# Seven quarter products for eight: one level of Strassen's algorithm in tiles three to nine of a chunked attention and feed-forward kernel

## The chip, the cores and the metric

The kernel runs on one core of a Trainium2 chip. The metric is the device time of one execution in microseconds (us). A core has a matrix engine (TensorE, PE in the profile, with its weight loads as PEld), VectorE (DVE), ScalarE (ACT), GpSimd (POOL) and SyncE (SP). Matmuls write to PSUM, in banks of 128 partitions by 512 floats; the other operands live in SBUF; DMA queues move data between SBUF and DRAM.

## The reference

Attention is computed in chunks of 64 tokens for 8 batches, 8 heads, 576 tokens and a head width of 64. Its output, seen as 4608 tokens by 512 features, goes through a feed-forward block of 2048 hidden units:

```python
scores = (1 / sqrt(64)) * matmul(q_c, k_c.T)          # 64 x 64 in each chunk
attn = exp(scores - max(scores)); attn = attn / (sum(attn) + 1e-09)
x = matmul(attn, v_c)                                 # as 4608 x 512
h = x @ w_in                                          # 512 x 2048
g = where(h >= 1, h, where(h <= -1, 0, (h + 1)**2 / 4))
out = g @ w_out                                       # 2048 x 512
```

The feed-forward weights come in as 64-bit floats; everything else is float32.

## The kernel before

**Tiles.** Tokens are worked in nine tiles of 512 (`NTILE`, `T`). In each tile there are four attention groups of two heads (`NP`) and 16 blocks of 128 hidden units (`NF`). Features run down the partitions: x of a tile is four blocks of 128 features by 512 tokens, one from each attention group.

**Precision.** Matmuls work on a reduced format (float32r), so each operand is split into a high part (a cast, on ScalarE) and a low part (the difference, on VectorE). A product is three matmuls: high by high, high by low, low by high. The split of x is `attn_split` (L513 to L526), that of the hidden units `ffn_split` (L554), and that of the weights happens once, in `prepare` (L250 to L294), which also turns 64-bit floats into 32-bit ones. All 16 + 16 prepared weight blocks stay in SBUF.

**The feed-forward block.** `ffn_in` (L529) does, for a block j, 12 matmuls of 512 columns (four feature blocks by three products, L539) into one of two PSUM banks `ps_h`; then ScalarE (L546, L549) and VectorE (L550) compute the activation. `ffn_out` (L564) runs two blocks behind (`LAG`): for each of four slices of 128 tokens three matmuls (L574), accumulated over the 16 blocks in four PSUM banks `ps_o`. `store` (L584) drains these and sends them out.

**Attention** of a group is prepared one or two groups ahead: 32-by-32 turns of q and k on VectorE (L375; in tile 0 on TensorE), scores (L399), softmax on VectorE and ScalarE (`attn_softmax`, L444), a DMA that finishes the turn of the weights (L499; on SyncE's queue, in tile 1 on GpSimd's), then the values product (L421), and the split of x for the next tile.

**Order.** Nothing is issued directly: every step is `plan.add(engine, cost, ...)`, with what it reads and writes. `Plan.emit` (L61) then walks a model of the engines in time and puts each engine's instructions into a fixed order: of the steps that are ready on an engine, the one added first goes first. On the chip each engine then runs its queue strictly in that order, and waits where data are not there. Queues are those of TensorE, ScalarE, VectorE, GpSimd (in tiles 0 and 1 some loads and transfers) and SyncE (all other DMAs). The filler matmuls of the start (L717, L720) keep TensorE busy while the first data arrive.

**The main loop** (L670 on) goes over tiles t and blocks j; the weights are prepared during tile 0, two at each j.

Of the kernel before, what the change touches and what calls it, by code (L numbers as in the profile page):

```python
# [17 lines left out]
class Plan:  # L18
# [8 lines left out]

    def __init__(self):
        self.parts = []
        self.writer = {}  # L30
        self.readers = {}

    def add(
        self, engine, cost, emit, reads=(), writes=(), lag=0.0, columns=0, port=False, moving=0.0
    ):
# [25 lines left out]
    def emit(self, filler):  # L61
# [25 lines left out]
        for _ in range(len(parts)):  # L87
            while True:
                best = None
                for e in engines:  # L90
                    while soon[e] and soon[e][0][0] <= free[e]:
                        heapq.heappush(now[e], heapq.heappop(soon[e])[1])
                    if now[e]:
                        start = free[e]
                    elif soon[e]:
                        start = soon[e][0][0]
                    else:
                        continue
                    if best is None or start < best[0]:
                        best = start, e  # L100
                start, e = best
                if filling and free[fill_engine] < start and fill_emit():
                    free[fill_engine] = self.products_end(free[fill_engine], fill_cost, fill_columns)
                    continue
                break
            while soon[e] and soon[e][0][0] <= start:
                heapq.heappush(now[e], heapq.heappop(soon[e])[1])
            n = heapq.heappop(now[e])
# [21 lines left out]
def kernel(  # L130
# [53 lines left out]
    xh_bufs = [buffers(sb, f"xh{g}_", 2, F32R) for g in range(NP)]  # L184
    xl_bufs = [buffers(sb, f"xl{g}_", 2, F32R) for g in range(NP)]
    r_bufs = buffers(sb, "r", 2)
    gh_bufs, gl_bufs = buffers(sb, "gh", 2, F32R), buffers(sb, "gl", 2, F32R)
    tmp_bufs = buffers(sb, "tmp", 4)
# [322 lines left out]
            plan.add(queue, 4.8, move, (xkey,), (akey,), lag=1.7, moving=0.4)  # L511

    def attn_split(t, g):  # L513
        pkeys, pair = bank_pair_of(t, g)
        hkey, xh = xh_bufs[g][t % 2]
        lkey, xl = xl_bufs[g][t % 2]

        def of_tokens(x):
            split = "p (r n q) -> p r n q" if t == 0 else "p (n r q) -> p r n q"
            return x.rearrange(split, r=2, q=C)  # L520

        ps = pair[:, :, HALF:].rearrange("p r (n q) -> p r n q", q=C)
        plan.add("act", 0.48, lambda: nc.scalar.copy(out=of_tokens(xh), in_=ps), pkeys, (hkey,))  # L523
        plan.add("dve", 0.6, lambda: nc.vector.tensor_tensor(  # L524
            out=of_tokens(xl), in0=ps, in1=of_tokens(xh.bitcast(F32)), op=ALU.subtract
        ), (*pkeys, hkey), (lkey,))  # L526
# [27 lines left out]
    def ffn_split(t, j):  # L554
        n = t * NF + j
        rkey, r = r_bufs[n % 2]
        ghkey, gh = gh_bufs[n % 2]
        glkey, gl = gl_bufs[n % 2]
        plan.add("act", 0.52, lambda: nc.scalar.copy(out=gh, in_=r), (rkey,), (ghkey,))  # L559
        plan.add("dve", 0.6, lambda: nc.vector.tensor_tensor(  # L560
            out=gl, in0=r, in1=gh.bitcast(F32), op=ALU.subtract
        ), (rkey, ghkey), (glkey,), port=True)

    def ffn_out(t, j):  # L564
        n = t * NF + j
        ghkey, gh = gh_bufs[n % 2]
        glkey, gl = gl_bufs[n % 2]
        for s in range(NS):
            pkey, acc = o_banks[s]

            def products(s=s, acc=acc):
                cols = slice(s * P, (s + 1) * P)
                for i, (x, half) in enumerate(((gh, 0), (gh, 1), (gl, 0))):
                    nc.tensor.matmul(  # L574
# [9 lines left out]
    def store(t, s):  # L584
# [15 lines left out]

        plan.add("sp", 0.6, send, (okey,), (), lag=1.7, moving=0.8)


    order = [("wi", 0), ("wi", 1)]
    for j in range(NF):
# [61 lines left out]
        11: ((back, 2),), 13: ((back, 3), (front, 4)),  # L667
    }
    LAG = 2
    for t in range(NTILE + 1):  # L670
        for j in range(NF):
            n = (t + 1) * NP + j // 4

            def attention():
# [5 lines left out]
                if j % 4 == 2:  # L680
                    if n + 1 < ALL:
                        attn_products(values_of(*now), scores_of(*then), lag=0.8)
                        attn_split(*now)
                        attn_softmax(*then)
# [8 lines left out]
                    what(*divmod(NP + g, NP))  # L693
            else:
                attention()
            if t < NTILE:
                ffn_in(t, j)
            prepare_next()
            prepare_next()
            m = t * NF + j - LAG  # L700
            if 0 <= m < NTILE * NF:
                ffn_out(*divmod(m, NF))
            if t < NTILE:
                ffn_split(t, j)

    zeros = place("zeros", "wo", 11, [P, 2, T], F32R)[:, 0, :]
    nc.vector.memset(zeros.bitcast(F32), 0.0)
# [60 lines left out]
```

## Time and profile before

| what | us |
|---|---|
| median of three runs | 877.92 (877.04 to 878.34) |
| the profiled execution | 879.29 |
| its span, first to last instruction | 877.5 |
| TensorE busy in the span | 858.6 |
| VectorE, ScalarE, GpSimd busy | 454.0, 377.6, 31.0 |
| matmuls of the h products (L539), high and low x | 384.0 and 224.5 |
| matmuls of the output products (L574), high and low | 356.0 and 224.3 |

Busy time of groups of matmuls overlaps, since one begins while the one before still drains. The mean granted TensorE clock is 0.997. In the profile's rows of groups stand line, engine, operation, out<-in, shapes and count, then busy time and mean duration in ns, then idle time before them and what ended it. DMA moved 63.94 MB in all, GpSimd's own queue 2.10 MB of it.

### The profile page before, as it was taken

What the parts mean: (1) busy time and instruction counts of PE and PEld (TensorE: products, weight loads), DVE (VectorE), ACT (ScalarE), POOL (GpSimd) and SP (SyncE); (2) the same over time, 40 slices, a digit from 0 to 9 for tenths busy, and PEclk for the clock granted to TensorE, in tenths of its full rate; (3) what the DMA queues carried; (4) which work ended last, traced back from release to release, by engine and by line L of the source; (5) the groups of instructions that cost most, each with busy time, mean ns of one, the idle gap of its engine ahead of it and who ended that gap; (6) DMA issues with size and microseconds to landing.
All of it is one profiled execution on the core that took longest, in us unless ns stands there. A gap on an engine that the chain in (4) does not pass through costs nothing.

```text
span 877.5 us, 15042 instructions
## 1 busy us (share of the span) xinstructions
PE 858.6 (98%) x5918; PEld 705.0 (80%) x5918; DVE 454.0 (52%) x775; ACT 377.6 (43%) x691; POOL 31.0 (4%) x58
## 2 busy tenths in 40 slices
PE   6998999999999999999999999999999999999998
PEld 6777778888888888888888888888888888888886
DVE  4899998444444445444544454444444444423222
ACT  4888875333433333333433343333333433333332
POOL 5123100000000000000000000000000000000000
PEclk9999999999999999999999999999999999999999
DMA  9889924222322223222322233222222311001001
GB/s 215 219 249 239 246 37 105 48 42 46 87 49 49 49 49 97 49 49 49 96 49 46 46 80 62 47 43 78 52 47 43 79 37 25 13 1 49 0 1 49
DMA packets 207304, 63.94 MB, mean 73 GB/s; under 512 B 184448, under 2 KB 199808, under 8 KB 207232
## 3 DMA queue, kind: packets, MB, share of 16 engines
q1 hardware_dynamic: 204640, 60.60, 29.9%
q0 software_dynamic: 1536, 2.10, 0.9%
q8 instruction: 47, 0.77, 0.4%
q10 hardware_dynamic: 1056, 0.26, 0.2%
q14 instruction: 25, 0.20, 0.1%
HBM read 45.09 MB, written 9.44 MB: 62 GB/s over the span
## 4 chain that ended last, share of the span: by engine, by line
PE 86%; DVE 6%; SPq 3%; DMA 2%; ACT 1%; issue 1%; DVEq 0%; ACTq 0%
PE ps_h L539 42%; PE ps_o L574 41%; PE ps_a L421 2%; SPq L308 2%; PE ps_a L399 2%; DVE tmp L271 1%; DVE tmp L276 1%; DMA words_wi<-in_moe_w_in_dram 1%; SPq L239 1%; DMA q_sb<-in_q_dram 1%; DVE parts_wo L290 1%; DVE tmp L264 1%; DVE r L550 1%; DVE gl L560 0%; DVE parts_wi L290 0%
## 5 line engine op out<-in xcount | busy, mean ns | idle before, releaser
L539 PE MATMUL ps_h<-xh,parts_wi 128*128 128x512 f32 x1152 | 384.0, 393 | 0.8 <-DVE parts_wi L290 0.4
L574 PE MATMUL ps_o<-parts_wo,gh 128*128 128x512 f32 x1152 | 356.0, 390 | 0.0
L539 PEld LDWEIGHTS ps_h<-xh,parts_wi 128*128 128x128 f32 x1152 | 216.1, 188 | 48.0 <-DVE parts_wi L290 0.9
L574 PEld LDWEIGHTS ps_o<-parts_wo,gh 128*128 128x128 f32 x1152 | 216.6, 188 | 45.2 <-DVE parts_wo L290 0.2
L550 DVE SCALAR_TENSOR_TENSOR r<-ps_h,r 128x512 f32<-128x512 f32 x144 | 97.8, 679 | 263.5 <-ACT r L549 263.5
L539 PE MATMUL ps_h<-xl,parts_wi 128*128 128x512 f32 x576 | 224.5, 390 | 0.0
L574 PE MATMUL ps_o<-parts_wo,gl 128*128 128x512 f32 x576 | 224.3, 389 | 0.0
L546 ACT ACTIVATE r<-ps_h 128x512 f32<-128x512 f32 x144 | 86.3, 599 | 266.0 <-PE ps_h L539 266.0
L559 ACT CAST gh<-r 128x512 fp32r<-128x512 f32 x144 | 89.7, 623 | 153.4 <-PE ps_o L574 113.3
L560 DVE TENSOR_TENSOR gl<-r,gh 128x512 fp32r<-128x512 f32 x144 | 98.2, 682 | 108.0 <-ACT gh L559 108.0
L574 PEld LDWEIGHTS ps_o<-parts_wo,gl 128*128 128x128 f32 x576 | 108.4, 188 | 22.5
L539 PEld LDWEIGHTS ps_h<-xl,parts_wi 128*128 128x128 f32 x576 | 108.2, 188 | 21.4
L549 ACT ACTIVATE r<-r 128x512 f32<-128x512 f32 x144 | 91.1, 632 | 3.4
L523 ACT CAST xh<-ps_a 128x512 fp32r<-128x512 f32 x34 | 20.0, 589 | 39.7 <-DVE mx L455 39.2
L421 PEld LDWEIGHTS ps_a<-aT,v_sb 64*64 64x64 f32 x1056 | 19.2, 136 | 15.5 <-issue 10.2
L480 DVE TENSOR_REDUCE sm<-e 128x8 f32<-128x512 f32 x30 | 20.6, 686 | 21.2 <-ACT e L474 20.3
L421 PE MATMUL ps_a<-aT,v_sb 64*64 64x64 f32 x1056 | 23.7, 227 | 4.1 <-ACT e L464 4.1
L524 DVE TENSOR_TENSOR xl<-ps_a,xh 128x512 fp32r<-128x512 f32 x34 | 23.5, 690 | 1.7 <-ACT xh L523 0.8
L455 DVE TENSOR_REDUCE mx<-ps_a 128x8 f32<-128x512 f32 x34 | 23.4, 688 | 0.6 <-PE ps_a L399 0.5
L507 DVE STREAM_TRANSPOSE x<-e 128x512 f32<-128x512 f32 x32 | 22.7, 710 | 0.9
L399 PE MATMUL ps_a<-kT,qT 64*64 64x64 f32 x1056 | 21.6, 219 | 1.2 <-DVE kT L375 1.2
L375 DVE STREAM_TRANSPOSE qT<-q_sb 128x512 f32<-128x512 f32 x32 | 22.4, 701 | 0.0
(80 smaller groups left out, 400.0 us busy)
## 6 DMA issues: line engine op xcount, KB each, us to landing
words_wi<-in_moe_w_in_dram SPq DMA_DIRECT2D x16, 512.0 KB, 5.8
words_wo<-in_moe_w_out_dram SPq DMA_DIRECT2D x16, 512.0 KB, 6.3
v_sb<-in_v_dram SPq DMA_DIRECT2D x128, 64.0 KB, 2.4
out_dram<-tmp SPq DMA_DIRECT2D x32, 256.0 KB, 2.0
q_sb<-in_q_dram SPq DMA_DIRECT2D x112, 64.0 KB, 2.4
k_sb<-in_k_dram SPq DMA_DIRECT2D x112, 64.0 KB, 2.4
aT<-x SPq DMA_DIRECT2D x224, 32.0 KB, 1.9
aT<-x POOLq DMA_DIRECT2D x32, 32.0 KB, 5.6
```

Source lines behind the costliest of these rows:

```text
L399: nc.tensor.matmul(out=pair[i * C:(i + 1) * C, half, place:place + C], lhsT=qT[rows, at], rhs=kT[rows, at], start=True, stop=True,)
L421: nc.tensor.matmul(out=pair[h * C:(h + 1) * C, half, HALF + n * C:HALF + (n + 1) * C], lhsT=v_sb[rows, of:of + C], rhs=aT[rows, at:at + C] ...
L455: plan.add("dve", 0.6, lambda: nc.vector.tensor_reduce(out=mx4, in_=sc, axis=AX.X, op=ALU.max), pkeys, (mkey,))
L507: plan.add("dve", 0.6, lambda: nc.vector.transpose(out=x.rearrange("p (e c q) -> p c e q", e=2, q=Q), in_=e.rearrange("p (c e q) -> p c e ...
L524: plan.add("dve", 0.6, lambda: nc.vector.tensor_tensor(out=of_tokens(xl), in0=ps, in1=of_tokens(xh.bitcast(F32)), op=ALU.subtract), (*pkey ...
L539: nc.tensor.matmul(out=ps, lhsT=weight["wi", j][:, half, kc * P:(kc + 1) * P], rhs=x, start=(kc == 0 and i == 0), stop=(kc == KC - 1 and i ...
L546: plan.add("act", 0.48, lambda: nc.scalar.activation(out=r, in_=ps, func=AF.Relu, bias=0.5, scale=0.5), (pkey,), (rkey,))
L549: plan.add("act", 0.52, lambda: nc.scalar.square(out=r, in_=r), (), (rkey,))
L550: plan.add("dve", 0.6, lambda: nc.vector.scalar_tensor_tensor(out=r, in0=ps, scalar=1.0, in1=r, op0=ALU.max, op1=ALU.min), (pkey,), (rkey,))
L559: plan.add("act", 0.52, lambda: nc.scalar.copy(out=gh, in_=r), (rkey,), (ghkey,))
L560: plan.add("dve", 0.6, lambda: nc.vector.tensor_tensor(out=gl, in0=r, in1=gh.bitcast(F32), op=ALU.subtract), (rkey, ghkey), (glkey,), port ...
L574: nc.tensor.matmul(out=acc, lhsT=x[:, cols], rhs=weight["wo", j][:, half, :], start=(j == 0 and i == 0), stop=(j == NF - 1 and i == 2),)
```

## The change

In tiles 2 to 8 ("three to nine") the product h = x @ w_in is done by one level of Strassen's algorithm in Winograd's form. A pair of hidden blocks (2p, 2p + 1) and the tile's 512 tokens are cut in two by two: hidden blocks in two, tokens in two halves of 256, features in even and odd groups of 128 (so that each half is two blocks of 128 features). Instead of eight quarter products there are seven, each of some sum of weight quarters by some sum of x quarters.

- **Weights.** In tile 1 `combine_weights` forms the four sums of quarters of a pair on VectorE, splits them into high and low parts in two staging tiles, and GpSimd's queue writes all seven operands of the pair (three are unsummed quarters) to DRAM: 8 pairs x 7 DMAs of 256 KB.
- **Reuse of SBUF.** The weight blocks `wi0` to `wi15` are handed over, two after each pair: to sets of x operands, to five ring slots of 512 KB, to a tile for h, one for partial sums, and a third buffer for the hidden units.
- **Streaming.** In tiles 2 to 8 each ring slot holds the weights of two products; `load_combos` loads it on GpSimd's queue, 196 times.
- **x.** `combine_x` takes the place of `attn_split` for tiles 2 on: a copy from PSUM to SBUF, sums of halves on VectorE, and their splits, 256 or 512 wide. It is added to the plan after the next group's softmax, not before.
- **Products.** `quarter` does six matmuls of 256 columns into one of the two `ps_h` banks. `ffn_quad` runs the seven of a pair, each drained by one addition on VectorE with a partial sum in SBUF (the first by a copy on ScalarE, the sixth by two additions), and puts the eight output groups of the pair before among them. The activation now reads h from SBUF.
- **Order.** `plan.add` gets `ahead`: a step with it goes before steps that were added up to that many places earlier. The additions and the copy have 100.

```diff
         self.parts.append((engine, cost, emit, needs, lag, columns, port, moving, writes))
+        self.turn.append((n - ahead, n))
...
-                        heapq.heappush(now[e], heapq.heappop(soon[e])[1])
+                        heapq.heappush(now[e], self.turn[heapq.heappop(soon[e])[1]])
...
     def attn_split(t, g):
+        if t > 1:
+            combine_x(t, g)
+            return
...
+    RING = 5
...
+    def combine_x(t, g):
+        i = g // 2
...
+        act_copy(
+            0.48, lambda: raw[name]().rearrange("p (n r q) -> p r n q", r=2, q=C), lambda: ps,
+            pkeys, (name,),
+        )
+        sub = ALU.subtract
+        if g % 2 == 0:
+            dve(0.34, sub, part(ta, 0), part(xe, 1), part(xe, 0), ("xe",), ("ta",))
+            act_copy(0.3, part(h0, 0), part(xe, 0), ("xe",), (h0k,))
+            act_copy(0.3, part(h0, 1), part(ta, 0), ("ta",), (h0k,))
+            dve(0.34, sub, part(l0, 0), part(xe, 0), plain(part(h0, 0)), ("xe", h0k), (l0k,))
+            dve(0.34, sub, part(l0, 1), part(ta, 0), plain(part(h0, 1)), ("ta", h0k), (l0k,))
+            return
+        dve(0.34, sub, part(tb, 0), part(xo, 1), part(ta, 0), ("xo", "ta"), ("tb",))
+        dve(0.34, sub, part(tb, 1), part(xo, 1), part(xe, 1), ("xo", "xe"), ("tb",))
+        dve(0.34, sub, part(ta, 1), part(xo, 0), part(tb, 0), ("xo", "tb"), ("ta",))
+        act_copy(0.52, h1, xo, ("xo",), (h1k,))
+        dve(0.6, sub, l1, xo, plain(h1), ("xo", h1k), (l1k,))
+        act_copy(0.52, h2, tb, ("tb",), (h2k,))
+        dve(0.6, sub, l2, tb, plain(h2), ("tb", h2k), (l2k,))
+        act_copy(0.3, part(m, 0), part(ta, 1), ("ta",), (mk,))
+        dve(0.34, sub, part(m, 1), part(ta, 1), plain(part(m, 0)), ("ta", mk), (mk,))
+
+    def combine_weights(p):
...
+        for j, ks, key, w in zip(js, keys, (k1, k2), (w1, w2)):
+            dve(0.6, ALU.add, fixed(w), lambda j=j: weight["wi", j][:, 0, :].bitcast(F32),
+                lambda j=j: weight["wi", j][:, 1, :].bitcast(F32), ks, (key,))
...
+        dve(0.34, ALU.add, fixed(two(s12, 0)), fixed(a21), fixed(a22), (k2,), (k12,))
+        dve(0.34, ALU.subtract, fixed(two(s12, 1)), fixed(two(s12, 0)), fixed(a11), (k1,), (k12,))
+        dve(0.34, ALU.subtract, fixed(two(s34, 0)), fixed(a11), fixed(a21), (k1, k2), (k34,))
+        dve(0.34, ALU.subtract, fixed(two(s34, 1)), fixed(a12), fixed(two(s12, 1)), (k1, k12), (k34,))
+        for n, (key, ap) in enumerate(((k12, s12), (k34, s34))):
...
+            act_copy(0.52, fixed(hi), fixed(ap), (key,), (hkey,))
+            dve(0.6, ALU.subtract, fixed(lo), fixed(ap), fixed(hi.bitcast(F32)), (key, hkey), (lkey,))
...
+        for r, src, reads in (
+            (0, of_block(0, 0), keys[0]), (1, of_block(0, 1), keys[0]), (6, of_block(1, 1), keys[1]),
+            (2, of_stage(0, 1), st[0]), (3, of_stage(0, 0), st[0]),
+            (5, of_stage(1, 0), st[1]), (4, of_stage(1, 1), st[1]),
+        ):
...
+                nc.gpsimd.dma_start(out=dst.bitcast(F32), in_=ap.bitcast(F32))
+
+            plan.add("pool", 0.7, send, reads, (f"dram{d}_{n}",), lag=1.7, moving=0.8)
+
+    def load_combos(d):
...
+            nc.gpsimd.dma_start(
+                out=held[ap].bitcast(F32), in_=combos[d % len(combos)].bitcast(F32)
+            )
...
+        plan.add("pool", 0.8, emit, (f"dram{n}_0", f"dram{n}_1"), (key,), lag=1.7, moving=1.5)
+
+    def quarter(t, p, r):
+        step = (t - 2) * NQ * 7 + 7 * p + r
+        d, n = divmod(step, 2)
+        while loaded["n"] < min(d + RING, LOADS):
+            load_combos(loaded["n"])
+            loaded["n"] += 1
+        pkey, ps = h_banks[step % 2]
...
+            w = held[f"ring{d % RING}"][:, n, :]
+            for i, (_, hi, lo) in enumerate(ops):
+                for k, (x, y) in enumerate(((0, hi), (0, lo), (1, hi))):
+                    at = (2 * x + i) * P
+                    nc.tensor.matmul(
+                        out=ps[:, :QC], lhsT=w[:, at:at + P], rhs=y(),
+                        start=i == 0 and k == 0, stop=i == 1 and k == 2,
+                    )
+
+        plan.add("pe", 0.72, emit, (f"ring{d % RING}", *(k for ks, _, _ in ops for k in ks)), (pkey,),
+                 columns=6 * QC)
...
+    def ffn_quad(t, p):
...
+        def add(out, product, name):
+            (pkey, ps), (skey, ap), (okey, o) = product, snap(name), into(out)
+            plan.add("dve", 0.36, lambda: nc.vector.tensor_tensor(
+                out=o(), in0=ps, in1=ap(), op=ALU.add
+            ), (pkey, skey), (okey,), ahead=100)
...
+        product = quarter(t, p, 0)
+        key, ap = snap("a")
+        act_copy(0.3, ap, fixed(product[1]), (product[0],), (key,), ahead=100)
+        add("h00", quarter(t, p, 1), "a")
+        out_products(2)
+        add("u", quarter(t, p, 2), "a")
+        out_products(1)
+        add("w", quarter(t, p, 3), "u")
+        out_products(1)
+        add("h01", quarter(t, p, 4), "w")
+        activate(0)
+        out_products(1)
+        product = quarter(t, p, 5)
+        add("v", product, "u")
+        add("h11", product, "w")
+        out_products(2)
+        add("h10", quarter(t, p, 6), "v")
+        activate(1)
+        out_products(1)
...
+            if t == 1:
...
+                if j % 2 == 1:
+                    combine_weights(j // 2)
+                    hand_over(j - 1)
+                    hand_over(j)
```

More of the change, by code (lines that the diff above doesn't have):

```diff
@@ L29, in __init__ @@
         self.parts = []
+        self.turn = []
         self.writer = {}
@@ L33, in add @@
     def add(
-        self, engine, cost, emit, reads=(), writes=(), lag=0.0, columns=0, port=False, moving=0.0
+        self, engine, cost, emit, reads=(), writes=(), lag=0.0, columns=0, port=False, moving=0.0,
+        ahead=0,
     ):
@@ L556, in ffn_split, with high, low, ffn_out @@
         rkey, r = r_bufs[n % 2]
[L557 to L568, printed above, removed]
+        ghkey, _, glkey, _ = g_of(t, j)
+        def high():
+            nc.scalar.copy(out=g_of(t, j)[1], in_=r)
+        def low():
+            _, gh, _, gl = g_of(t, j)
+            nc.vector.tensor_tensor(out=gl, in0=r, in1=gh.bitcast(F32), op=ALU.subtract)
+        plan.add("act", 0.52, high, (rkey,), (ghkey,))
+        plan.add("dve", 0.6, low, (rkey, ghkey), (glkey,), port=True)
+    def ffn_out(t, j, *some):
+        ghkey, _, glkey, _ = g_of(t, j)
+        for s in some or range(NS):
             pkey, acc = o_banks[s]
             def products(s=s, acc=acc):
+                _, gh, _, gl = g_of(t, j)
                 cols = slice(s * P, (s + 1) * P)
@@ L601, in store, with take, emit @@
         plan.add("sp", 0.6, send, (okey,), (), lag=1.7, moving=0.8)
+    QC = T // 2
+    NQ = NF // 2
+    RING = 5
+    held = {}
+    def take(name, tags, shape, dtype, keys):
+        old = [f"{w}{j}_{n}" for w, j in tags for n in range(2)] if tags[0][0] == "wi" else list(tags)
+        def emit():
+            tag = f"{tags[0][0]}{tags[0][1]}" if tags[0][0] == "wi" else tags[0]
+            held[name] = sb.tile(shape, dtype, name=name, tag=tag)
+        plan.add("pool", 0.0, emit, (), (*old, *keys))
@@ new lines, in unit, with fixed @@
+    def unit(name, n):
+        return lambda: held[name][:, n, :]
+    def fixed(ap):
+        return lambda: ap
+    raw = {}
+    for g, name in enumerate(("xe", "xo", "ta", "tb")):
+        raw[name] = lambda name=name: held[name]
+    SNAPS = {"a": (0, 0), "u": (0, 1), "v": (1, 0), "w": (1, 1)}
+    units = [[], []]
+    for i in range(7):
+        units[0] += [(f"x0_{2 * i + n}", unit(f"set{i}", n)) for n in range(2)]
+    units[1] = [
+        *((f"xh{g}_1", fixed(xh_bufs[g][1][1])) for g in range(NP)),
+        *((f"xl{g}_1", fixed(xl_bufs[g][1][1])) for g in range(NP)),
+        *((f"xl{g}_0", fixed(xl_bufs[g][0][1])) for g in range(NP)),
+        ("x1_0", unit("set7", 0)), ("x1_1", unit("set7", 1)),
+    ]
@@ new lines, in act_copy, with dve, part, plain @@
+    def act_copy(cost, out, src, reads, writes, ahead=0):
+        plan.add(
+            "act", cost, lambda: nc.scalar.copy(out=out(), in_=src()), reads, writes, ahead=ahead
+        )
+    def dve(cost, op, out, one, two, reads, writes):
+        plan.add("dve", cost, lambda: nc.vector.tensor_tensor(
+            out=out(), in0=one(), in1=two(), op=op
+        ), reads, writes, port=True)
+    def part(ap, n):
+        return lambda: ap()[:, cols(n)]
+    def plain(ap):
+        return lambda: ap().bitcast(F32)
@@ L604, with g_of @@
+    def g_of(t, j):
+        n = t * NF + j
+        if t < 2:
+            return *gh_bufs[n % 2], *gl_bufs[n % 2]
+        if n % 3 < 2:
+            return *gh_bufs[n % 3], *gl_bufs[n % 3]
+        return "gh2", held.get("g3") and held["g3"][:, 0, :], "gl2", held.get("g3") and held["g3"][:, 1, :]
     order = [("wi", 0), ("wi", 1)]
@@ L695 @@
                 attention()
-            if t < NTILE:
-                ffn_in(t, j)
+            if t > 1 and j % 2 == 0:
+                p = j // 2
+                if t < NTILE:
+                    ffn_quad(t, p)
+                elif j == 0:
+                    for n in range(2):
+                        ffn_out(t - 1, NF - 2 + n)
+            if t > 1:
+                continue
+            ffn_in(t, j)
             prepare_next()
```

124 lines of the change are left out of this document (116 added, 8 removed).

## Prediction

> **What bounds the kernel now.** I read the page's list of engines first, then a table by stage, then the chain that ended last for one round of the steady part.
>
> ```profile
> span 877.5 us, 15042 instructions
> PE 858.6 (98%) x5918; PEld 705.0 (80%) x5918; DVE 454.0 (52%) x775; ACT 377.6 (43%) x691; POOL 31.0 (4%) x58
> ...
> 30.00:134.00 104.00, 96.83 (x745) 77.41 (x744) 101.07 (x192) 85.98 (x204) 16.98 (x33) 0.98 0.73 190
> 134.00:226.50 92.50, 92.50 (x643) 76.02 (x642) 50.00 (x84) 35.99 (x61) 0.00 (x0) 1.00 0.31 65
> 226.50:318.80 92.30, 92.30 (x642) 75.86 (x641) 44.56 (x75) 34.56 (x58) 0.00 (x0) 1.00 0.26 55
> ...
> 562.38 2.95 PE ps_h L539 x12
> 565.33 2.72 PE ps_o L574 x12
> 568.05 2.72 PE ps_h L539 x12
> ...
> 585.46 2.95 PE ps_h L539 x12
> ```
>
> The columns of the stage rows are length, then PE, PEld, DVE, ACT and POOL busy, granted clock, DMA share and GB/s. The first row is tile 0: VectorE is busy 101.07 of 104 us there, preparing weights. Then come tile 1 and tile 2: TensorE is busy all the time, VectorE about half. The chain is nothing but matmuls: 12 for h (L539, 2.72 us), 12 for the output (L574, 2.72 us), in turn. A round (four h blocks and one attention group) lasts 585.46 - 562.38 = 23.08 us, so a tile 92.3 us. Tiles 2 to 8, which the change rewrites, hold the time from about 226.5 us to the end: 651 us. So matmul time counts at its full price there, and work on other engines costs nothing until it makes TensorE wait.
>
> **The h products.** One block is 12 matmuls of 512 columns in 2.72 us, 226.7 ns each. A pair of blocks takes 24 of them, 5.44 us. The change makes seven products of six matmuls, 256 columns wide: 42 matmuls. What one costs decides the sum. If it were just half, 42 x 113.4 ns = 4.76 us. But each comes with its own weight load, and the load is as large as before. The warm-up filler has such matmuls, 256 wide, each with its load; three answers of the timeline give starts in one run of them, and two more a run 128 wide (start, length of the merged run, count):
>
> ```profile
> 20.41 0.40 PE L720 MATMUL ps_h<-zeros_wo 128*128 128x256 f32 x2
> 20.53 0.64 PE L720 MATMUL ps_h<-zeros_wo 128*128 128x256 f32 x4
> 20.88 0.46 PE L720 MATMUL ps_h<-zeros_wo 128*128 128x256 f32 x2
> 7.19 1.06 PE L717 MATMUL ps_h<-ident 128*128 128x128 f32 x8
> 7.97 0.28 PE L717 MATMUL ps_h<-ident 128*128 128x128 f32 x1
> ```
>
> The second row's four begin at 20.53 and the last of them is the one that starts at 20.88: three steps in 0.35 us, and from 20.41 four in 0.47, 118 ns each. The 128-wide run has eight, from 7.19 to the last one's start at 7.97: seven steps of 111 ns, though half the columns: the load is the floor there, and 256 columns sit just above it. I take 119 ns: 42 x 0.119 = 5.00 us a pair, 0.44 saved. There are 8 pairs in each of 7 tiles: **56 x 0.443 = 24.8 us off**. The ends are 113.4 ns (38 us off) and 125 (11 off). Output products and attention keep their matmuls.
>
> The Trainium skill ("TensorE: Matmul & The Clock Gate", Part 3, "What overlaps and what doesn't") says that a weight load overlaps matmuls in flight only when it goes to another row group. All these loads fill the whole array, so by that rule load and stream would add up. The trace disagrees: 226.7 ns for 512 columns has no room for a load of 111 beside a stream of 213.
>
> **What VectorE and ScalarE add in tiles 2 to 8.** Durations include a tail that the next instruction covers, so I use the step between neighbours:
>
> ```profile
> 540.72 0.69 DVE L524 TENSOR_TENSOR xl<-ps_a,xh 128x512 fp32r<-128x512 f32 x1
> 541.33 0.68 DVE L471 TENSOR_TENSOR e<-ps_a,mx 128x512 f32<-128x512 f32 x1
> 541.92 0.70 DVE L375 STREAM_TRANSPOSE kT<-k_sb 128x512 f32<-128x512 f32 x1
> L480 DVE TENSOR_REDUCE sm<-e 128x8 f32<-128x512 f32 x4 | 2.7, 686 | 2.6 <-ACT e L474 2.5
> L481 DVE TENSOR_SCALAR sm<-sm 128x8 f32<-128x8 f32 x4 | 0.7, 173 | 0.1
> ```
>
> A 512-wide operation steps by 0.60 us. No 256-wide one is shown; it lies between L481 and L480, and a straight line between their durations gives 173 + 513 x 248/504 = 425 ns, a step of about 0.34. Per pair VectorE then has seven additions (2.4) and four operations as before (2.4), 4.8 us. Per attention group the softmax and turns stay (seven operations of 0.6 and two small ones, 4.7), and the high/low split of 0.6 becomes 1.0 in an even group (three at 0.34) and 2.6 in an odd one (four at 0.34, two at 0.6). A tile: 8 x 4.8 + 4 x 6.5 + 1.2 for stores = 66 us of the new 88.8: 74% where it was 48%. ScalarE gains a 0.3 us copy a pair and 0.6 to 1.4 us a group: 34.6 + 2.4 + 4 = 41 of 88.8. So VectorE stays off the bound on average; what can hurt is the wait. A product writes one of two ps_h banks, and the product after next waits until it is drained; behind that wait stands all of TensorE's queue. How fast a drain starts:
>
> ```profile
> 541.86 0.39 PE L539 MATMUL ps_h<-xh,parts_wi 128*128 128x512 f32 x1
> 542.09 0.62 PE L574 MATMUL ps_o<-parts_wo,gh 128*128 128x512 f32 x2
> 542.29 0.60 ACT L546 ACTIVATE r<-ps_h 128x512 f32<-128x512 f32 x1 [1.60 <-PE ps_h L539]
> ```
>
> 0.20 us after TensorE has moved on. With 0.43 for the addition, a drain is done at about 0.65. Between a product and the one that reuses its bank lie one or two output groups (0.68 each) and another product (0.71): 1.4 us at the tightest place (after the seventh), 2.1 or more elsewhere. A 0.6 us operation ahead of the addition still fits, and the planner now ranks additions ahead of up to 100 earlier parts. I cost this at 0; uncovered, it costs up to one such operation a group, 0.6 x 28 = 17 us.
>
> The split, moved behind the next group's softmax, is needed only by the next tile. Attention's own chain gets longer on a busier VectorE. It has room: transposes go out at 546.51 and the next values products come at 561.22 (561.22 - 546.51 - 5.02 = 9.7 us for a landing that takes 1.9):
>
> ```profile
> 546.51 5.02 SPq L499 DMA_DIRECT2D aT<-x  x8
> 561.22 0.69 PE L421 MATMUL ps_a<-aT,v_sb 64*64 64x64 f32 x32
> aT<-x SPq DMA_DIRECT2D x224, 32.0 KB, 1.9
> ```
>
> **The stream of weights.** 196 loads of 512 KB go through GpSimd's queue into five slots. A load feeds two products; a pair takes 5.00 + 5.44 = 10.44 us for 3.5 loads: one each 2.98 us, 176 GB/s beside the 55 of now. A slot comes free after its second product and is needed four slots later: cover 4 x 2.98 = 11.9 us. Each load waits on GpSimd for its slot; behind it stand only later loads, and TensorE waits for those.
>
> ```profile
> 50.00:60.00 10.00, 8.81 (x68) 7.00 (x67) 8.95 (x17) 6.64 (x16) 3.80 (x8) 1.00 1.01 338
> words_wo<-in_moe_w_out_dram SPq DMA_DIRECT2D x16, 512.0 KB, 6.3
> aT<-x POOLq DMA_DIRECT2D x32, 32.0 KB, 5.6
> L341 POOL DMA_DIRECT2D v_sb<-in_v_dram x8 | 5.0, 636 | 0.2 <-issue 0.2
> L499 POOL DMA_DIRECT2D aT<-x x32 | 15.9, 507 | 56.4 <-issue 44.9 <-DVE x L507 11.5
> ```
>
> 231 GB/s is under the 338 that one stretch moved, a 512 KB load landed in 6.3 us while the engines were busy, and GpSimd's own queue landed in 5.6. Issue takes 0.5 to 0.64 us each. So I cost it at 0, hidden by matmuls.
>
> **Tile 1, once.** Eight sums of weights: per pair four 512-wide and four 256-wide VectorE operations, 3.8 us, 30 in all, and 56 DMAs of 256 KB (0.6 to 0.8 us of GpSimd each, 14.7 MB). VectorE had 50 of 92.5 busy: it fits, at about 85%. ScalarE's copy into the staging tile waits for the previous pair's transfers (5.6 us by the GpSimd row), and behind it stand the activations that TensorE needs. The 24 unsummed quarters depend only on prepared weights, so they can leave in tile 0. There they share GpSimd's queue with 32 attention transfers (L499) that wait for VectorE, and a send behind one waits too; DMA is 0.73 busy, and a few waits for loads are on the chain:
>
> ```profile
> 48.05 4.01 DMA words_wo<-in_moe_w_out_dram
> 82.73 5.01 DMA q_sb<-in_q_dram
> ```
>
> Below: 0, or a little gained if order shifts. Above: 2.4 us for each of eight pairs, 19. I take 3, nearer the hidden end, because the activations run ahead of their use: the block that ended at 542.09 has its last piece at 547.04,
>
> ```profile
> 546.39 0.65 DVE L560 TENSOR_TENSOR gl<-r,gh 128x512 fp32r<-128x512 f32 x1
> ```
>
> and its output products come after four more runs of 2.72 us, at 552.97: 5.9 us to spare. The tail adds 0.6: the last block's activation has 2.7 us of output products to hide behind, not 5.4.
>
> **Sum.** Profiled execution 879.3 (span 877.5 and 1.8 around it): 879.3 - 24.8 + 3 + 0.6 = 858.1. The median is 1.4 lower: **856.7 us**.
>
> **Rivals.**
> Forecast, 849 to 863: 0.55.
> Half-price matmuls (113 to 116 ns), 841 to 849: 0.05. For it, only that 512-wide ones run at 0.443 ns a column; against it, the six steps above.
> Given back by waits (a blocked drain each group, 17 us, or the staging wait in tile 1, 19 us), 863 to 876: 0.17. For it, VectorE at 74 to 85% in a fixed order; against it, the covers above.
> Seven cost as much as eight, no change, 876 to 880: 0.07. It needs 24 x 226.7 / 42 = 129.5 ns a matmul, or both kinds of wait whole. The filler multiplies zeros; real operands are not shown.
> Slower, **the stream starves the five slots**, over 880: 0.12. Place: the wait of a product on its slot. It decides at a pace: a load each 2.98 us hides, 2.98 + 24.8/196 = 3.11 us loses the whole gain, and at 3.3 us the time is 858 + 196 x 0.32 = 920. For it: GpSimd's queue moved 2.1 MB so far, never 512 KB at once, and attention's transfers in small pieces hold a DMA share of 0.26 for 55 GB/s. Against it: 338 GB/s above.
> Other losses in tiles 0 and 1 beyond 19 us, slower too: 0.03.
> Loads that do not overlap matmuls: 111 + 113 = 224 ns a matmul, 9.4 us a pair, 56 x 4.0 = 222 us longer, 1080: 0.01. The Trainium skill's sentence on row groups says this.
>
> **Range.** 843 to 881 holds the forecast, most of the cheaper case, the third and the fourth: about 0.83. Measurement can tell some 0.2%, 1.8 us: faster 0.77, same 0.07, slower 0.16.
>
> **What would show it.** Right: 256-wide ps_h matmuls stepping at 117 to 121 ns, a round of about 22.2 us, TensorE without gaps from tile 2 on, VectorE near 75%, loads landing within 8 us. Wrong: matmuls waiting for DMA into the slots (the stream), for a VectorE addition (the banks), or ScalarE waiting for DMA in tile 1 (staging). A round of 23.08 without gaps would mean that the matmul's price is wrong.

## The result and the profile after

The changed kernel takes **863.84 us** (median of four runs, 861.88 to 863.85) against 877.83 of the kernel before in the same comparison: a ratio of 0.9836, interval 0.9819 to 0.9853. It is 14.0 us faster. The forecast was 856.7, 21 us faster: direction right, a third of the gain missing. 863.84 lies inside the wide range of 843 to 881, but 0.8 us above the forecast's own range (849 to 863) and in the band of the rival "given back by waits". As the trace shows, it is not there by that rival's mechanism: the waits it names do not occur. In the experiments below, one execution of the version without reloading took 1665.1 us and is left out of its figures.

The profiled execution took 863.85 us. The page's span and list of engines:

```profile
span 862.0 us, 18545 instructions
...
PE 844.2 (98%) x6926; PEld 735.8 (85%) x6926; DVE 652.5 (76%) x1329; ACT 436.8 (51%) x833; POOL 176.1 (20%) x310
```

The table by stage (length, then PE, PEld, DVE, ACT and POOL busy, clock, DMA share, GB/s) for tile 0, tile 1 and tile 2:

```profile
30.00:134.00 104.00, 97.15 (x773) 77.44 (x774) 101.14 (x191) 85.61 (x202) 33.79 (x55) 0.98 0.91 244
134.00:226.50 92.50, 92.50 (x642) 76.02 (x641) 83.27 (x164) 49.67 (x87) 25.49 (x37) 1.00 0.62 180
226.50:318.80 92.30, 92.30 (x798) 82.10 (x798) 68.13 (x144) 42.03 (x78) 14.85 (x28) 1.00 0.75 210
```

TensorE still has no gap in tile 1 or tile 2: matmuls remain the bound. The granted clock is 1.00 in both. VectorE is at 68.13 of 92.30 in tile 2, 74% as forecast, ScalarE at 42. The DMA's pace is 210 GB/s where 231 had been worked out.

One pair of hidden blocks in the chain that ended last (start, us, what):

```profile
400.61 0.71 PE ps_h L802 x6
401.32 0.69 PE ps_o L594 x3
...
404.83 0.71 PE ps_h L802 x6
405.54 1.39 PE ps_o L594 x6
406.93 0.71 PE ps_h L802 x6
407.64 0.69 PE ps_o L594 x3
...
410.50 2.07 PE ps_o L594 x9
```

A product of six narrow matmuls takes 0.71 us, so seven take 4.98, as forecast (5.00). But an output group, the same three wide matmuls as before, takes 0.69 us here where twelve took 2.72 (0.68 a group). The run of nine shows it from within: its third group adds 2.07 - 1.39 = 0.68, the first two 1.39 together. Something at the start of each run of wide matmuls costs time. The steps from one matmul's start to the next, by place in the run, worked out from the trace's start times from 230 us on (means in ns, waits left out, runs behind attention left out):

```
place in the run            1      2      3      4      5      6      7
before: 512 wide          226.7  226.7  226.5  226.7  226.7  226.5  226.7
after: 512 behind 256     233.3  235.8  228.3  232.6  230.8  226.6  227.5
after: 256 behind 512     115.5  118.6  119.5  120.5  117.9  118.4  119.9
```

The first five wide matmuls behind narrow ones are each 1.6 to 9 ns longer. Three lose 17 ns, six or more 27. Summed over the 1367 wide output matmuls from 230 us on, the excess over 226.7 is **6.7 us**; the narrow ones are 0.5 us under 119 ns.

The stream and the drains, in the page's rows of groups and of DMA issues (the last number is the median landing):

```profile
L779 POOL DMA_DIRECT2D ring<-combos x196 | 103.8, 530 | 528.5 <-PE ps_h L802 513.0
...
L824 DVE TENSOR_TENSOR h<-ps_h,snaps 128x256 f32<-128x256 f32 x224 | 93.8, 419 | 55.0 <-PE ps_h L802 52.7
...
ring<-combos POOLq DMA_DIRECT2D x196, 512.0 KB, 4.2
```

GpSimd waits for TensorE to free a slot nearly all the time, and VectorE's additions wait for TensorE: both run ahead. TensorE's matmuls wait for neither: their view of waits from 226 to 850 us lists nothing.

A round (one attention group and two pairs) takes 22.39 us, 23.08 before, but 22.62 where a tile begins. The timeline there (start, us, engine, line; idle time before and what ended it in brackets):

```profile
327.72 0.59 ACT L610 COPY tmp<-ps_o 128x512 f32<-128x512 f32 x1 [0.70 <-PE ps_o L594]
...
328.36 0.53 PEld L594 LDWEIGHTS ps_o<-parts_wo,g 128*128 128x128 f32 x3 [0.17 <-ACT tmp L610]
328.36 0.97 PE L594 MATMUL ps_o<-parts_wo,g 128*128 128x512 f32 x3
```

The last output group of the old tile, for the fourth slice of tokens, waits for ScalarE's copy, which drains the *third* slice. These lie in two banks of one buffer, and the order is kept per buffer. Seven such places at 0.235 us: 1.6 us.

**Balance.** Profiled, 863.85 less the forecast 858.1 leaves 5.75 us. Wide matmuls after a change of width +6.7; tile starts +1.6; narrow matmuls -0.5; tiles 0 and 1 took less than the 3 us allowed: the first attention group of tile 1 starts at 147.2 us, at 145.8 before, so -1.6. Sum +6.2, 0.45 too much. The runs behind attention groups, which the table leaves out, account for that: before the change, wide h products lost 25 ns in their first steps at 24 places from tile 2 on (the steps stand under "Mis-sized" below), and the forecast did not count these 0.6 us among what it removed. That leaves 0.15 us the other way. The median of before lay 1.4 under its profiled execution and that of after does not, which makes 7.1 between the medians' forecast and result.

### The profile page after: what moved, and what is told of

The parts are those of the page before. It is cut to its first block, busy times and chain, and to the rows that moved or that the text cites. A ratio compares the mean times of both kernels' runs of the same rounds, so it can differ in the third digit from the quotient of the medians.

```text
span 862.0 us, 18545 instructions
## 1 busy us (share of the span) xinstructions
PE 844.2 (98%) x6926; PEld 735.8 (85%) x6926; DVE 652.5 (76%) x1329; ACT 436.8 (51%) x833; POOL 176.1 (20%) x310
## 4 chain that ended last, share of the span: by engine, by line
PE 85%; DVE 7%; SPq 5%; DMA 1%; issue 1%; ACT 1%; DVEq 0%
PE ps_o L594 43%; PE ps_h L802 33%; PE ps_h L555 6%; PE ps_a L434 2%; SPq L335 2%; SPq L321 2%; PE ps_a L412 1%; DVE tmp L284 1%; DVE tmp L289 1%; DMA k_sb<-in_k_dram 1%; DVE r L566 1%; SPq L252 1%; SPq L259 1%; DVE tmp L277 1%; DVE parts_wo L303 0%
## 5 line engine op out<-in xcount | busy, mean ns | idle before, releaser
L594 PE MATMUL ps_o<-parts_wo,gh 128*128 128x512 f32 x848 | 267.2, 396 | 0.0
L802 PEld LDWEIGHTS ps_h<-set,ring 128*128 128x128 f32 x1464 | 204.4, 189 | 15.9
L802 PE MATMUL ps_h<-set,ring 128*128 128x256 f32 x1464 | 217.5, 283 | 0.0
L779 POOL DMA_DIRECT2D ring<-combos x196 | 103.8, 530 | 528.5 <-PE ps_h L802 513.0
L824 DVE TENSOR_TENSOR h<-ps_h,snaps 128x256 f32<-128x256 f32 x224 | 93.8, 419 | 55.0 <-PE ps_h L802 52.7
L594 PE MATMUL ps_o<-parts_wo,g 128*128 128x512 f32 x456 | 123.4, 394 | 0.0
L835 DVE SCALAR_TENSOR_TENSOR r<-h,r 128x512 f32<-128x512 f32 x112 | 76.9, 687 | 29.0 <-ACT r L834 28.9
L555 PE MATMUL ps_h<-xh,parts_wi 128*128 128x512 f32 x256 | 87.2, 398 | 0.8 <-DVE parts_wi L303 0.4
L594 PEld LDWEIGHTS ps_o<-parts_wo,g 128*128 128x128 f32 x456 | 78.5, 189 | 10.9 <-ACT tmp L610 0.3
L555 PEld LDWEIGHTS ps_h<-xh,parts_wi 128*128 128x128 f32 x256 | 48.1, 188 | 12.2 <-DVE parts_wi L303 0.9
```

Of the source, the lines that this page charges most:

```text
L555: nc.tensor.matmul(out=ps, lhsT=weight["wi", j][:, half, kc * P:(kc + 1) * P], rhs=x, start=(kc == 0 and i == 0), stop=(kc == KC - 1 and i ...
L594: nc.tensor.matmul(out=acc, lhsT=x[:, cols], rhs=weight["wo", j][:, half, :], start=(j == 0 and i == 0), stop=(j == NF - 1 and i == 2),)
L779: nc.gpsimd.dma_start(out=held[ap].bitcast(F32), in_=combos[d % len(combos)].bitcast(F32))
L802: nc.tensor.matmul(out=ps[:, :QC], lhsT=w[:, at:at + P], rhs=y(), start=i == 0 and k == 0, stop=i == 1 and k == 2,)
L824: plan.add("dve", 0.36, lambda: nc.vector.tensor_tensor(out=o(), in0=ps, in1=ap(), op=ALU.add), (pkey, skey), (okey,), ahead=100)
L835: plan.add("dve", 0.6, lambda: nc.vector.scalar_tensor_tensor(out=r, in0=held["h"][:, f, :], scalar=1.0, in1=r, op0=ALU.max, op1=ALU.min), ...
```

## Experiments

Each ratio is to the kernel before, on the same chip. "The mark" is the start of the first attention group in tile 1 (145.8 before, 147.2 after).

**Is it the stream?** Only the first five of 196 loads are issued; all later products then use weights that are not theirs.

```diff
         def emit():
+            if d >= RING:
+                return
             nc.gpsimd.dma_start(
```

> The changed kernel without the reloading of its five ring slots: only the first five of 196 loads are issued, so later products use stale weights. Theory A (the stream is hidden; output matmuls lost their even step to the narrow products among them): no difference over 1 us, output groups stay at 0.693 us. Theory B (the stream's writes into SBUF slow the output matmuls from 0.680 to 0.693 us a group): 448 groups x 0.013 = 5.8 us faster, 858. Theory C (products wait for late loads): faster by those waits, which the trace of the changed kernel puts under 1 us.

Measured 861.97 (median of three), ratio 0.9811 (0.9794 to 0.9828). The chain at the place shown above:

```profile
399.91 0.69 PE ps_o L594 x3
400.60 0.71 PE ps_h L804 x6
401.31 0.69 PE ps_o L594 x3
```

Rounds are 22.38 and 22.63, as with the stream. The span is 2.9 us shorter, all of it ahead of the mark (144.4), where the streamed loads have not begun: the mark varies by that much between layouts of this kernel (144.4 to 148.6 in the runs of this study that left tile 0's work alone). From the mark on, the stream costs nothing, and the slow output groups are not its doing.

**Does a wide matmul pay for a narrow one ahead of it?** The kernel before, with the h products of tiles 2 to 8 done 256 wide: twice as many matmuls, no stream, no new VectorE work.

```diff
+            c, kc = slice(part // KC * HALF, (part // KC + 1) * HALF), part % KC
...
+                    nc.tensor.matmul(
+                        out=ps[:, c], lhsT=weight["wi", j][:, half, kc * P:(kc + 1) * P],
+                        rhs=x[:, c], start=(kc == 0 and i == 0), stop=(kc == KC - 1 and i == 2),
+                    )
```

> The kernel before, with the 12 matmuls of 512 columns of an h block done as 24 of 256 in tiles 2 to 8, and nothing else: no stream, no sums, no additions on VectorE. Theory A (a narrow matmul costs 0.119 us by itself and unsettles the next six wide ones by 27 ns in all): an h block 2.86 in place of 2.72 us, its output block 2.75 in place of 2.72, 112 blocks x 0.167 = 18.7 us slower, 896.5. Theory B (narrow matmuls cost half a wide one and the rest comes from stream or VectorE): no change, 878. A without the unsettling: 112 x 0.14 = 15.7 slower, 893.5.

Measured 897.41, ratio 1.0214 (1.0196 to 1.0233). Its chain:

```profile
408.41 2.75 PE ps_o L589 x12
411.16 2.87 PE ps_h L554 x24
414.03 2.75 PE ps_o L589 x12
416.78 2.87 PE ps_h L554 x24
```

The twelve output matmuls, untouched, take 2.75 us where they took 2.72. Their steps are 233.4, 235.9, 228.3, 232.5, 230.8 and then 226.7 ns: the series of after, without Strassen. The round grows from 23.08 to 23.75, (23.75 - 23.08)/4 = 0.168 us a block. The chain's pieces give the same: 2.87 - 2.72 for the narrow ones and 2.75 - 2.72 for the wide ones behind them, 0.18, less 0.01 because narrow ones lose a little less behind attention. Without the slow first steps of the wide ones (their settling) it would have been 0.15, 893.5 in all.

**Fewer or more changes of width.** The same products and groups in another order: the eight output groups of a pair in three runs (3, 3, 2), or all in one.

```diff
-        out_products(2)
+        out_products(3)
         add("u", quarter(t, p, 2), "a")
-        out_products(1)
         add("w", quarter(t, p, 3), "u")
-        out_products(1)
+        out_products(3)
...
-        out_products(1)
```

> The changed kernel with the eight output groups of a pair in three runs (3, 3, 2) in place of six (2, 1, 1, 1, 2, 1): in tiles 2 to 8, 168 runs of six or nine matmuls in place of 212 of three and 112 of six or nine. Theory A (each run loses 17 ns if it has three matmuls, 27 if six or more): 168 x 27 = 4.5 us in place of 212 x 17 + 112 x 27 = 6.6, so 2.1 us faster, 861.7. Theory B (wide matmuls are slower throughout, whatever the order): the same as the changed kernel within 0.5 us. Theory C (the two banks no longer cover the drains when two products stand together): slower, with matmuls waiting for VectorE.

> The changed kernel with all eight output groups of a pair added behind its seven products; the planner then puts 55 runs of 24 matmuls. Theory A alone: 55 x 27 ns = 1.5 us lost in place of 6.6, 5.1 us faster, 858.7. Theory C (drains decide once nothing lies between products): a product of 0.71 us leaves 0.71 for a drain of 0.65 that needs VectorE at once; with one 0.6 us operation ahead it waits about 0.55, some two to four times a pair, 56 pairs x 1.1 to 2.2 = 60 to 120 us slower. With VectorE's other work moved beside the output runs by the planner the waits may shrink to some 0.2 us a pair, 11 us slower.

Three runs: 874.51, ratio 0.9956 (0.9942 to 0.9970). One run: 915.79, ratio 1.0426 (1.0411 to 1.0441); there the output groups stand behind both activations, so half of them take hidden units of the next pair, and this version computes something else. Three runs, TensorE and then VectorE in the timeline:

```profile
319.86 0.88 PE L802 MATMUL ps_h<-set,ring 128*128 128x256 f32 x6
...
322.05 0.62 PE L802 MATMUL ps_h<-xh,ring 128*128 128x256 f32 x3 [0.60 <-DVE h L824]
```

```profile
320.38 0.69 DVE L835 SCALAR_TENSOR_TENSOR r<-h,r 128x512 f32<-128x512 f32 x1
320.98 0.71 DVE L388 STREAM_TRANSPOSE qT<-q_sb 128x512 f32<-128x512 f32 x1
321.61 0.39 DVE L824 TENSOR_TENSOR h<-ps_h,snaps 128x256 f32<-128x256 f32 x1
```

The product begun at 319.86 was done at 320.57; its addition came at 321.61, behind an activation and a turn of q. The third product in a row needs that bank and waits. In one run of eight, the view of waits for TensorE:

```profile
PE ps_h L802 <- DVE h L824: 12.4, 29, 0.9
PE ps_h L802 <- DVE snaps L824: 2.6, 12, 0.2
```

The same view of the weight loads gives 25.4 and 11.7 us for these two. So with products in a row the drains are no longer hidden; the groups that stand between products hide them. The gain from fewer changes of width can't be had this way.

**Pairs of products, never three.** Four output runs of two groups each.

```diff
         out_products(2)
         add("u", quarter(t, p, 2), "a")
-        out_products(1)
         add("w", quarter(t, p, 3), "u")
-        out_products(1)
+        out_products(2)
         add("h01", quarter(t, p, 4), "w")
         activate(0)
-        out_products(1)
```

> The same products and output groups in another order: two products, two output groups, two products, two, two products, two, one product, two. No three products stand together, and each reuse of a ps_h bank has two output groups and at least one product between, 2.1 us. Theory, settling of the wide matmuls: 223 runs of six cost 27 ns each, 6.0 us, against 212 x 17 + 112 x 27 = 6.6, and 100 fewer products begin with the short step of 115 ns, +0.4 us: no change, 863.8 within 1 us (ratio 0.984). Theory C in the narrow form, a drain decides only where three products stand together: no waits for a bank. In the wide form, where two do: waits of 0.2 to 0.8 us once or twice a round, 28 x 0.35 = 10 us later, 874 (0.996).

Measured 867.89, ratio 0.9881 (0.9863 to 0.9900): between the two forms of the theory. Three of four rounds take 22.78, one 22.39. VectorE in the timeline where one product ended at 288.27:

```profile
288.29 0.65 DVE L493 TENSOR_REDUCE sm<-e 128x8 f32<-128x512 f32 x1
288.97 0.17 DVE L494 TENSOR_SCALAR sm<-sm 128x8 f32<-128x8 f32 x1
289.18 0.20 DVE L495 RECIPROCAL sm<-sm 128x8 f32<-128x8 f32 x1
289.30 0.37 DVE L824 TENSOR_TENSOR snaps<-ps_h,snaps 128x256 f32<-128x256 f32 x1
```

The addition starts 1.03 us after TensorE has moved on, behind three softmax operations, and the next two products lose 0.39 us in four steps. At this place what decides is not how many products stand together, but which operations VectorE's fixed order puts ahead of the addition.

**The rank of the drains.** `ahead=0` in place of 100 for the additions and the copy.

> The additions and the copy that drain the products get no rank ahead of other steps; the planner, which models the drains, then also lays TensorE's work in longer runs (34 product runs of twelve and 24 longer ones after the reorder, where there were 56). Theory, the rank is what keeps the drains inside the cover: additions stand behind softmax steps of 0.6 us on VectorE and products wait for a bank, at least one such step a round, 28 x 0.6 = 17 us: about 881 (ratio 1.003), more where three or more products stand in a row without a group between them. Rival, the planner finds groups to put in between: 863.8 within 2 us (0.984).

Measured 882.95, ratio 1.0055 (1.0037 to 1.0072): the first theory's 881. Rounds are 22.97, 23.59, 22.97 and 23.83. TensorE in the timeline:

```profile
316.97 0.39 PE L594 MATMUL ps_o<-parts_wo,gl 128*128 128x512 f32 x1
317.44 1.70 PE L802 MATMUL ps_h<-set,ring 128*128 128x256 f32 x12
319.29 1.69 PE L802 MATMUL ps_h<-set,ring 128*128 128x256 f32 x12 [0.15 <-DVE snaps L824]
```

Twelve narrow matmuls take 1.85 us from start to start where 1.43 is the rule, and 0.47 stand between the last wide one's start and the first narrow one's where 0.23 is the rule. Without the rank, the change is slower than the kernel before. This is the "uncovered" 17 us of the prediction, at 19.1. TensorE's order changes with the rank, since the planner then lays products in longer runs (11 runs of eight, where the longest had been three), so the two were not separated. But the loss sits at the drains: from 140 us on the weight loads wait 14.7 and 3.9 us for VectorE's additions, and not at all in the changed kernel.

**Width, or operands and bank?** In tiles 2 to 8 the output products of blocks 1 to 14 are done 256 wide as well, so that width hardly ever changes.

```diff
+                width = HALF if t > 1 and 0 < j < NF - 1 else T
+                for c in range(0, T, width):
...
+                            out=acc[:, c:c + width], lhsT=x[:, cols],
+                            rhs=weight["wo", j][:, half, c:c + width],
```

> In tiles 2 to 8 the output products of hidden blocks 1 to 14 of 16 are done 256 columns wide, six matmuls to a group instead of three; everything else as after the change. Theory, it is the change of width that a wide matmul has to settle from: without it every step is 118 to 120 ns, a group 0.712 us where it is 0.693 with its settling, and no first product of 115 ns: 392 groups x 0.019 = 7.4 us and 0.4 for the firsts, 871.6 (ratio 0.993). Rival, it is the change of operands or of bank that costs the 17 to 27 ns of a run: they stay on top, 7.4 + 6 = 13 us, 877 (0.999). Rival, settling is nothing of its own and wide matmuls cost 231 ns flat in this kernel: then no difference between the first steps of a run and the later ones is left to lose, and the group is again 0.712: the time cannot tell it from the first theory, the steps in the trace can.

Measured 875.99, ratio 0.9977 (0.9968 to 0.9986): nearer the rival's 877 than the 871.6. TensorE in the timeline says otherwise:

```profile
269.79 0.88 PE L805 MATMUL ps_h<-set,ring 128*128 128x256 f32 x6
270.51 0.40 PE L596 MATMUL ps_o<-parts_wo,gh 128*128 128x256 f32 x2
270.75 0.28 PE L596 MATMUL ps_o<-parts_wo,gl 128*128 128x256 f32 x1
...
271.95 0.88 PE L805 MATMUL ps_h<-set,ring 128*128 128x256 f32 x6
```

A product's six matmuls take 0.72 us, the twelve output matmuls 1.44: 120 ns each, at every place of a run and through both changes of operand, bank and accumulation. Where 512-wide ones are left (blocks 0 and 15), they again step by 233, 235 and 228. So it is the width. The time is 12.2 us over the changed kernel's because the flat step is 120, not 118 to 120: a group 0.720 instead of 0.693 and a product 0.720 instead of 0.711, which over some 14 narrowed groups and 14 products a round is 0.5 us (22.88 for 22.39).

**How much cover the stream needs.** Three ring slots, and two.

```diff
-    RING = 5
+    RING = 3
```

> Three ring slots in place of five. A slot comes free after its second product and is needed two slots later: cover 2 x 2.98 = 6.0 us against a landing of 4.2 and an issue of 0.5. Theory, the stream is hidden with room to spare: the time stays at 863.8 within 1 us (ratio 0.984), rounds 22.39. Rival, single loads that land late use up the five slots now and then: with three the late ones show, some 0.5 us in one load of five, 196 x 0.1 = 20 us, 884 (1.007).

> Two ring slots. A slot comes free after its second product and is needed again one slot later: cover 2.98 us less the issue of 0.5 against a landing of 4.2. The theory that the cover is what hides the stream has TensorE wait 4.2 + 0.5 - 2.98 = 1.7 us at each of 196 loads, 333 us, less what the landing gains from emptier queues (1.2 us: 240): 1100 to 1200 us (ratio 1.25 to 1.37). Rival, the planner's order or early issue hides it all the same: under 900.

Three: 867.14, ratio 0.9877 (0.9856 to 0.9898). Two: 920.01, ratio 1.0477 (1.0449 to 1.0505). TensorE's waits from 145 us on, with three and then with two:

```profile
PE ps_h L802 <- DMA ring<-combos: 2.0, 2, 1.7
```

```profile
PE ps_h L802 <- DMA ring<-combos: 31.8, 43, 1.8
```

With three, most rounds are 22.39 and a few late loads show, 3 us in all: more than nothing, less than the 20 of the rival. Five slots are not far more than needed. With two, the loss is (918.5 - 862.0)/196 = 0.29 us a load; 1.2 to 1.7 had been worked out. The planner also put more groups together there (57 runs of three or more groups for 11), which lengthens the cover; how much of the miss that explains was not separated. Of the 56 us over the version with five slots, 31.8 are the waits shown here. The trace also has three stretches of 3.4 us at a granted clock of 0.5 (from 326.5, 377.7 and 551.8 us), where the version with five slots has none; they can hold up to 5 us, an estimate (half of 10.2).

**Tile 0's 1.4 us.** The 24 sends of unsummed quarters wait for their pair's first sum, and so leave in tile 1.

```diff
-            (0, of_block(0, 0), keys[0]), (1, of_block(0, 1), keys[0]), (6, of_block(1, 1), keys[1]),
+            (0, of_block(0, 0), (*keys[0], f"go{js[0]}")), (1, of_block(0, 1), (*keys[0], f"go{js[0]}")),
+            (6, of_block(1, 1), (*keys[1], f"go{js[1]}")),
```

> The 24 DMAs of the unsummed quarters now wait for their pair's first weight sum, so that they leave in tile 1, not in tile 0. The first steady attention round stands at 147.2 us after the change and at 145.8 before it. If these DMAs in tile 0 (6.3 MB on top of a DMA share of 0.73) are what costs the 1.4 us, the mark comes back to about 145.8 and the time falls by 1 to 2 us, to about 862.4 (ratio 0.982). Rival: the mark varies with every layout of the kernel (144.4 to 148.6 so far) and the DMAs cost nothing: no change from 863.8 (0.984) within 1.5 us. Rival: tile 1's queue becomes too full, since GpSimd then issues 56 DMAs in 92 us and the hand-over of the blocks waits: 0.5 to 1.5 us later for each pair, 868 to 876 (0.989 to 0.998).

Measured 862.97, ratio 0.9835 (0.9795 to 0.9876): not to be told from the changed kernel. The mark came back to 144.8, but 1.9 us were lost at the end of tile 1. Its SyncE timeline there, and then that of the changed kernel:

```profile
202.79 10.16 SPq L512 DMA_DIRECT2D aT<-x  x8
```

```profile
202.91 5.93 SPq L512 DMA_DIRECT2D aT<-x  x8
```

And its row of tile 1 in the table by stage:

```profile
134.00:226.50 92.50, 90.94 (x635) 74.66 (x634) 80.89 (x159) 48.36 (x85) 41.06 (x58) 1.00 0.77 240
```

Eight issues took 10.16 us for 5.93, with DMA at 240 GB/s in tile 1 for 180, and the values product waited 1.6 us for the last. Whether the 2.4 us of tile 0 are the sends' or its usual variation stays open. The granted clock may hold part of them: in tile 0 it is 0.5 for 3.4 us twice in the changed kernel's trace (from 13.7 and 78.5 us), and once in the trace of before (76.5) and in this one (76.8). Such a stretch can cost at most 1.7 us, an estimate (half of it). The clock alone does not set the mark, which stood at 145.6 and 146.4 in two versions without any (four output runs, 256-wide output products).

**The attention transfers of tile 1 on SyncE's queue,** on top of the last one.

```diff
-        queue = "pool" if t == 1 else "sp"
+        queue = "sp"
```

> As with the late quarters (24 DMAs of unsummed quarters leave in tile 1), and the attention transfers of tile 1 go on SyncE's queue instead of GpSimd's. The late quarters brought the first steady attention round from 147.2 to 144.8 us and gave 1.9 us back at the end of tile 1, where the values product waited 1.6 us for an attention transfer. Theory, that transfer stood behind the sends in GpSimd's queue: on the other queue the wait goes, the mark stays at about 144.8, and the time is 863.0 - 1.9 = 861.1 (ratio 0.981). Rival, it is DMA bandwidth or SyncE's own loads that hold it: the wait stays, 863 (0.983).

Measured 875.43, ratio 0.9970 (0.9958 to 0.9981): 12 us worse, and the premise was wrong. Attention runs a tile ahead: the transfers that waited at the end of tile 1 serve tile 2 and were on SyncE's queue already, as the two SyncE lines above show. What moved were the 32 transfers for tile 1, which go out in tile 0, where SyncE issues most of the loads. TensorE's waits there, from 20 to 165 us:

```profile
PE ps_a L434 <- DMA aT<-x: 11.9, 4, 5.0
PE ps_a L412 <- DVE kT L388: 2.7, 1, 2.7
```

The mark moves to 159.2.

**The wait at a tile's start.** On top of that, the second and third slice take the shared pair of banks.

```diff
-            pkey, acc = o_banks[s]
+            pkey, acc = o_banks[(0, 2, 3, 1)[s]]
```

`store`, which drains them, has the same edit.

> As the version before, and the output groups of a tile's second and third slice use the two halves of the shared pair of ps_o banks, where the third and fourth did. In the round at each tile's start the fourth slice's group (328.36 us) waits for the copy that drains the third slice, though that lies in another bank: both banks are one buffer for the ordering. The second and third groups stand next to each other in the order, so no copy is issued between their matmuls. Theory: the round at a tile's start falls from 22.62 to 22.39 us, 7 x 0.235 = 1.6 us: 859.5 (ratio 0.979). Rival, the wait is for a drain that is really needed, or the order of the planner shifts and pays it elsewhere: 861.1 (0.981).

Measured 874.10, ratio 0.9955 (0.9943 to 0.9967), 1.3 us under the version it builds on, though the two intervals overlap; the rounds show the effect more surely than the time. The chain at the start of tile 3, and that of the changed kernel:

```profile
341.16 0.71 PE ps_h L803 x6
341.87 0.69 PE ps_o L594 x3
```

```profile
327.69 0.71 PE ps_h L802 x6
328.39 0.93 PE ps_o L594 x3
```

The group takes 0.69 us for 0.93, and every round of the steady part is 22.37 to 22.39. This edit was not run on the changed kernel alone; by these rounds it should bring it to about 862.2, an estimate.

## Why the prediction was right and where it was off

- **Right: the saving on the h products.** 42 matmuls were put at 0.119 us, 5.00 a pair; they take 4.98. That a 256-wide matmul with its own weight load sits a little above half a 512-wide one was read from the filler, and real operands agree. Within a run loads overlap matmuls: the steps are 115 to 121 ns (table above). They are not the 224 ns that would follow from the rule on row groups in the Trainium skill ("TensorE: Matmul & The Clock Gate", Part 3, "What overlaps and what doesn't"). The first step behind each of 24 attention groups is 223 ns. (The rival without overlap was put at 1080 us. Its 222 us come on top of the kernel before, so it should have read 1100.)
- **Right: the stream hides.** Removing it changes no round. The rival's mechanism is real, but with five slots it is out of reach; the version with two takes 56 us more than that with five.
- **Right, but on a thinner basis than argued: the drains hide.** VectorE's load was well forecast (74%), the cover of 1.4 us too. What holds it is the order: without the rank (and with the longer runs that follow from it), 19.1 us more; with the output groups in three runs, 10.7. The prediction's 17 us for it was a fair price.
- **Mis-sized: "Output products and attention keep their matmuls".** The matmuls were kept, their price wasn't. A group of 0.680 became 0.697 alone and 0.693 in a run of two, since each of the 324 output runs from tile 2 on now follows narrow matmuls: 6.7 us, more than the whole shortfall of the profiled time. Rows that hinted at it were in the trace of before: behind an attention group its first h matmuls step by 338, 231, 236, 228, 233 and 231 ns before they reach 227, which is part of why twelve take 2.95 us there and not 2.72. The prediction quoted 2.95 and 2.72 and made nothing of the difference, of which the five steps after the first are 25 ns.
- **Unforeseen: 1.6 us at tile starts.** Spreading the output groups among products lets a drain be issued between two groups that share a buffer. Before, the four groups stood together.
- **Over-estimated: tiles 0 and 1**, at 3 us for a measured 1.4; tile 1 keeps its 23.08 us rounds though VectorE is at 90% (85% forecast).

## What to carry to other kernels

When a change alternates matmuls of two shapes, take the price of the unchanged ones from a place in the trace where they stand behind another shape, not from their long runs. When drains of a two-bank rotation fall to a shared engine, check what its fixed order puts ahead of each drain; average load says little. And two banks declared as one buffer are one buffer to the ordering, however the work is spread.

## What the hardware showed

After a change from 256 to 512 columns the first five matmuls step by 233, 236, 228, 233 and 231 ns, the sixth by 227. The series is the same within 1 ns in the changed kernel and in the kernel before with 256-wide h products, with a stream beside it or none, and it does not appear with changes of operand, bank or accumulation at one width. Narrow ones among themselves step by a flat 120 ns; behind wide ones the first takes 113 to 116. The granted clock is 1.00 throughout. The first step behind the 64 x 64 matmuls of attention is longer, 338 ns at 512 columns in the kernel before and 223 at 256 in the changed one; a first step of 223 also stands behind the wait for a bank at 289.73 us of the version with four output runs. That is 103 to 111 ns more than the steady step, near the 111 ns that the prediction read for a weight load, which may not overlap there; this was not tried. What in TensorE or its weight loads makes the series of five was not tried either.
